# Attention masks per key block, two score rounds before two products with v, and an order of issue from a list scheduler

## The chip, the cores and the metric

The kernel runs on one core of a Trainium2 chip. The metric is device time in microseconds (us). A run of the kernel before takes 985 to 991 us, and the runs of one kernel mostly lie within 0.3% of their median (0.4% at most).

Engines in the profile: PE is TensorE's matrix products, PEld its weight loads, DVE is VectorE, ACT is ScalarE, POOL is GpSimd, SP is SyncE. A "q" after the name (SPq) is the engine's queue, which issues transfers.

## The reference, cut to what matters

```python
# attention: batch 4, 8 heads, 768 tokens, head size 64
q_bucket = sum over 6 bits of (q @ proj > 0) * 2**bit      # k_bucket likewise
scores = where(q_bucket == k_bucket, q @ k.T / 8, -1e9)
attn = exp(scores - max);  attn = attn / (sum(attn) + 1e-9)
x = attn @ v                                               # then (tokens, heads * 64)
# feed-forward: 3072 tokens, 512 -> 2048 -> 512
h = x @ w_in;  g = h * erf(softplus(h));  out = g @ w_out
```

The kernel does attention first (32 heads, two at a time: 16 pairs), then the feed-forward part. The mask is a matrix product too: bits of +1 and -1, with a large weight, are added into the scores before the exponential.

## The kernel before

A pair is four rounds `n`: two halves of the queries times two halves of the keys. A round has three key blocks `c` of 128 keys. All engines get their instructions in the order in which this program emits them, and each engine works its list off in that order; semaphores make an instruction wait for what it reads.

```python
def scores(n):                       # cut
    for part in range(2):            # part 0: masks, part 1: scores
        for c in range(GC):          # three key blocks
            for ab in range(2):      # the two heads of the pair
                rows = slice(ab * D, ab * D + D)
                ks, qs = d["k"][rows, :], d["q"][rows, :]
                if part == 0:
                    ks, qs = bit_rows(d, ab, c % 2)      # 32 rows of bits
                nc.tensor.matmul(out=d["st"][c][:, ab, 0:HS], lhsT=ks[:, keys], rhs=qs[:, cols],
                                 start=(part == 0), stop=(part == 1))
...
def invert(i):                       # after the divisor went through DRAM (zd, zc)
    nc.vector.reciprocal(out=zc, in_=zc)
    nc.sync.dma_start(out=rd..., in_=zc)
    for ab in range(2):              # spread over 64 rows each
        nc.sync.dma_start(out=d["r"][ab * D : ab * D + D, :], in_=rd[ab : ab + 1, :].broadcast_to([D, S]))

def normalise(i):                    # x = (x + ev) * r, on VectorE
    nc.vector.scalar_tensor_tensor(out=x, in0=x, scalar=d["ev"][:, 0:1], in1=d["r"], op0=ALU.add, op1=ALU.mult)
    nc.sync.dma_start(out=xs[b][j], in_=x)
...
for n in range(NS + 1):              # written out by hand, cut
    scores(n); exponentials(n)
    if ahead: hash_bits(pairs[i + 1], big)
    sum_keys(n - 1); weigh(n - 1)    # weigh: product with v of the round before
    if ahead: take_bits(pairs[i + 1], bitp)
    ...
    if r == 3 and i >= 1: invert(i - 1)
    if r == 1 and i >= 2: normalise(i - 2)
```

The divisor goes a long way: `z` leaves for DRAM as `zd`, comes back spread over 128 rows as `zc`, is inverted, leaves again as `rd`, and comes back as `r`, repeated for the 64 rows of each head. SyncE requests all four transfers.

Between these, ScalarE and VectorE convert the weights, one piece of 512 KB for every two rounds (`keep`, `top`, `unit`, `rest`), and VectorE adds up parts of them (presums).

Of the kernel before, what the change touches and what calls it, by code (L numbers as in the profile page):

```python
# [56 lines left out]
P = 128  # L58
# [88 lines left out]
def kernel(  # L147
# [36 lines left out]
    QR = 32  # L184
    proj_sb = const.tile([P, 2 * QR], F32, name="proj_sb")
    weight = const.tile([P, 1], F32, name="weight")
# [9 lines left out]
    most = const.tile([P, 2, B * H], F32, name="most")  # L196
    proj_in = const.tile([P, 2 * NBIT], F32, name="proj_in")
    nc.scalar.dma_start(out=proj_in, in_=proj2)
    nc.vector.memset(proj_sb, 0.0)
    for ab in range(2):  # L200
# [6 lines left out]
    nc.scalar.dma_start(out=row, in_=bucket)  # L207
    steps = const.tile([P, 3], F32, name="steps")
    nc.vector.tensor_scalar(
        out=steps[:, 0:1],  # L210
        in0=row,
        scalar1=float(QR),
        scalar2=-float(QR),
        op0=ALU.is_ge,
        op1=ALU.mult,
    )
    nc.vector.tensor_tensor(out=row, in0=row, in1=steps[:, 0:1], op=ALU.add)
    for c, (end, factor) in enumerate(((NBIT, NBIT + 1.0), (NBIT + 1, -float(NBIT)))):
        nc.vector.tensor_scalar(
            out=steps[:, c + 1 : c + 2],  # L220
            in0=row,
            scalar1=float(end),
            scalar2=factor * BIG,
            op0=ALU.is_lt,
            op1=ALU.mult,
        )
    nc.vector.tensor_tensor(out=weight, in0=steps[:, 1:2], in1=steps[:, 2:3], op=ALU.add)
    nc.vector.memset(ones, 1.0)
# [55 lines left out]
    def fetch(i, load):  # L284
        d = dict(
            q=load.tile([P, S], F32, name="q", tag="q"),
            k=load.tile([P, S], F32, name="k", tag="k"),
            v=load.tile([P, NC, P], F32, name="v", tag="v"),
        )
        b, j = divmod(i, JP)  # L290
        for n, what in enumerate("qk"):
            for ab in range(2):
                nc.sync.dma_start(
                    out=d[what][ab * D : ab * D + D, :],
                    in_=qkT[2 * i + ab, n * D : n * D + D, :],
                )
        for ab in range(2):
            nc.sync.dma_start(
                out=d["v"][:, :, ab * D : ab * D + D],
                in_=v[b, 2 * j + ab].rearrange("(c p) d -> p c d", p=P),  # L300
            )
        return d
# [14 lines left out]
    def take_bits(d, bitp, halves=(0, 1)):  # L317


        if halves[0] == 0:  # L320
            for what in ("qb", "kb"):
                d[what] = bitp.tile([P, S], BF16, name=what, tag=what)
        h0, h1 = halves[0], halves[-1] + 1
        cols = slice(h0 * HS, h1 * HS)
        nc.scalar.activation(
            out=d["qb"][:, cols].rearrange("p (h s) -> p h s", s=HS),
            in_=d["bits"][:, h0:h1, 0:HS],
# [4 lines left out]
        for half in (1, 0):  # L332
            nc.vector.tensor_scalar(
                out=d["kb"][half * D : half * D + D, cols],
                in0=d["qb"][D:P, cols],
                scalar1=weight[D:P, 0:1],
                scalar2=None,
                op0=ALU.mult,
            )
        nc.vector.tensor_copy(out=d["qb"][D:P, cols], in_=d["qb"][0:D, cols])  # L340

    def bit_rows(d, ab, copy):

        rows = slice(copy * D + ab * QR, copy * D + ab * QR + QR)
        return d["kb"][rows, :], d["qb"][rows, :]

    def attention():
        NS = NPAIR * 4
        with (
# [19 lines left out]
            def fetch_weights(n):  # L369
                if n >= len(pieces):  # L370
                    return
                queue = nc.sync if n < 2 else nc.gpsimd
# [8 lines left out]
            def round_weights(n, part):  # L381
# [5 lines left out]
                raw = raws[n]  # L387
                low, high = raw[:, :, 0], raw[:, :, 1]
                if part == 0:
                    keep = cvt.tile([P, WP], I32, name="keep", tag="keep")  # L390
                    top = cvt.tile([P, WP], I32, name="top", tag="top")
                    raws[n, 1] = keep, top
                    sq = keep[:, :].bitcast(F32)
                    nc.scalar.activation(out=sq, in_=high.bitcast(F32), func=AF.Square)  # L394
                    nc.scalar.activation(  # L395
                        out=keep, in_=sq, func=AF.Sign, scale=-1.0, bias=tiny2[:, 0:1]
                    )
                    nc.vector.tensor_scalar(
                        out=top,
                        in0=high,  # L400
                        scalar1=3,
                        scalar2=0x7FFFFFFF,
                        op0=ALU.logical_shift_left,
                        op1=ALU.bitwise_and,
                    )
                    nc.vector.scalar_tensor_tensor(
                        out=top,
                        in0=high,
                        scalar=SIGN,
                        in1=top,  # L410
                        op0=ALU.bitwise_and,
                        op1=ALU.bitwise_or,
                    )
                    return
                keep, top = raws.pop((n, 1))
                unit = cvt.tile([P, WP], I32, name="unit", tag="unit")
                rest = cvt.tile([P, WP], F32, name="rest", tag="rest")
# [4 lines left out]
                    in1=keep,  # L422
# [5 lines left out]
                )  # L428
                nc.vector.scalar_tensor_tensor(
# [10 lines left out]
                raws.pop(n)  # L440

            def scores(n):
# [3 lines left out]
                d["st"] = [big("st") for _ in range(GC)]  # L446
                for part in range(2):
                    for c in range(GC):
                        keys = slice((g * GC + c) * P, (g * GC + c + 1) * P)
                        for ab in range(2):  # L450
                            rows = slice(ab * D, ab * D + D)
                            ks, qs = d["k"][rows, :], d["q"][rows, :]
                            if part == 0:
                                ks, qs = bit_rows(d, ab, c % 2)
                            nc.tensor.matmul(  # L455
                                out=d["st"][c][:, ab, 0:HS],
                                lhsT=ks[:, keys],
                                rhs=qs[:, cols],
                                start=(part == 0),
                                stop=(part == 1),  # L460
                            )

            def exponentials(n):
                d = pairs[n // 4]
                for c, st in enumerate(d.pop("st")):
                    e = etiles[(n * GC + c) % len(etiles)]
                    nc.scalar.activation(  # L467
                        out=e[:, :, 0:HS], in_=st[:, :, 0:HS], func=AF.Exp, scale=scale
                    )

            def sum_keys(n):
                d = pairs[n // 4]
                key = "sum", n // 2 % 2
                es = [etiles[(n * GC + c) % len(etiles)][:, :, 0:HS] for c in range(GC)]
                if n % 2 == 0:
                    d[key] = sums.tile([P, 2, HS], F32, name="sum", tag="sum")
                    nc.vector.tensor_tensor(out=d[key], in0=es[0], in1=es[1], op=ALU.add)
                    es = es[2:]
                for e in es:
                    nc.vector.tensor_tensor(out=d[key], in0=d[key], in1=e, op=ALU.add)  # L480

            def weigh(n):
# [5 lines left out]
                for c in range(GC):  # L488
                    e = etiles[(n * GC + c) % len(etiles)]
# [13 lines left out]
            def divisor(n):  # L503
                half = n // 2 % 2
                d = pairs[n // 4]
                z = bank("z_ps")[:, 0:HS]
                for ab in range(2):
# [6 lines left out]
                    )  # L514
                if half == 0:
                    d["z"] = home(n // 4).tile([P, S], F32, name="z", tag="z")
                nc.scalar.copy(out=d["z"][:, half * HS : (half + 1) * HS], in_=z)

            def leave(n):

                half = n // 2 % 2
                d = pairs[n // 4]
                cols = slice(half * HS, (half + 1) * HS)
                if half == 0:
                    d["x"] = home(n // 4).tile([P, S], F32, name="x", tag="x", bufs=3 if n < NS - 4 else 1)
                nc.scalar.copy(out=d["x"][:, cols], in_=d["av"][:, 0:HS])
                if half == 0:
                    d["ev"] = small.tile([P, 1], F32, name="ev", tag="ev")
                    nc.vector.tensor_scalar(
                        out=d["ev"],  # L530
                        in0=d["av"][:, HS : HS + 1],
                        scalar1=EPS,
                        scalar2=None,
                        op0=ALU.mult,
                    )

            def spread(i):

                d = pairs[i]
                zd = dram.tile([2, S], F32, name="zd", tag="zd")  # L540
                d["zc"] = small.tile([P, 2 * S // P], F32, name="zc", tag="zc")
                for ab in range(2):
                    nc.sync.dma_start(out=zd[ab : ab + 1, :], in_=d["z"][ab * D : ab * D + 1, :])
                nc.sync.dma_start(
                    out=d["zc"],
                    in_=zd[:, :].rearrange("a (p c) -> (a p) c", c=2 * S // P),
                )

            def invert(i):
# [6 lines left out]
                rd = dram.tile([2, S], F32, name="rd", tag="rd")  # L556
# [685 lines left out]
```

## Time and profile before

| | before |
|---|---|
| median, us | 987 |
| attention: first mask to last product with v, us | 10.6 to 354.0 |
| one pair in the steady part, us | 21.38 |
| VectorE's busy time in a pair, us | 18.8 to 19.6 |
| ScalarE's, us | 14.1 |

The prediction below shows the busy shares, the stretches of two pairs and the order of time. A line of an order of time has the start in us, the length, the engine, the line of the program, the operation, out<-in, and in brackets how long the engine had been idle and what ended that.

The list of waits of the kernel before (engine, what it did, what it waited for: total us, times, longest) has it once in the whole run:

```profile
DVE x L571 <- DMA r<-rd: 1.5, 1, 1.5
```

### The profile page before, as it was taken

Reading aid. Unit: us, or ns where it says so; the run is one execution under the profiler, and the core shown is the slowest. Engines: PE = TensorE matmul, PEld = TensorE weight load, DVE = VectorE, ACT = ScalarE, POOL = GpSimd, SP = SyncE. Lnnn points to the kernel's source line nnn. Section 1 sums busy time; section 2 is a strip of 40 time slices with the busy share of each in tenths; the row PEclk is TensorE's granted clock in tenths of the full one; section 3 lists DMA queues with packets and bytes.
Section 4 is the critical chain, followed back from the end, with each engine's and each line's share of the span. In section 5 each row is a group of like instructions: output and inputs, shape, how many; then the busy total and the mean of one; then the engine's idle time right before and its main releaser. Section 6 shows DMA issues by size and latency. Waiting matters only on the chain.

```text
span 986.7 us, 11526 instructions
## 1 busy us (share of the span) xinstructions
PE 968.8 (98%) x4290; PEld 557.3 (56%) x4290; DVE 837.5 (85%) x1071; ACT 734.0 (74%) x866; POOL 16.2 (2%) x34
## 2 busy tenths in 40 slices
PE   7999999999999999999999999999999999999997
PEld 2444444444444467765666666666666666666543
DVE  3888898989998967989999999988998899888861
ACT  3676676666666637789889988988788889987960
POOL 0000000000000000000000000000000000000000
PEclk9999999999999999999999999999999999999999
DMA  8454556654555322211112102210221000000001
GB/s 187 111 126 124 145 140 154 144 160 125 126 144 139 120 92 80 76 33 32 49 46 88 33 28 85 70 33 16 75 74 33 1 22 22 1 1 21 22 1 45
DMA packets 61680, 74.54 MB, mean 76 GB/s; under 512 B 33936, under 2 KB 44176, under 8 KB 61616
## 3 DMA queue, kind: packets, MB, share of 16 engines
q1 hardware_dynamic: 57008, 57.99, 21.6%
q0 software_dynamic: 4320, 15.73, 5.3%
q8 instruction: 35, 0.57, 0.2%
q14 instruction: 29, 0.24, 0.1%
q10 hardware_dynamic: 288, 0.01, 0.0%
HBM read 60.92 MB, written 12.78 MB: 75 GB/s over the span
## 4 chain that ended last, share of the span: by engine, by line
PE 92%; ACT 4%; DVE 2%; issue 1%; DMA 1%; SPq 0%; DVEq 0%
PE o_ps L902 32%; PE X L791 16%; PE st L455 14%; PE av L492 13%; PE Z L791 8%; PE Y L791 4%; PE bits L309 3%; PE z_ps L508 2%; ACT e L467 1%; ACT keep L395 1%; ACT keep L394 1%; DVE s L876 1%; DMA k<-in_qkT_dram 0%; DVE s L852 0%; DVE s L846 0%
## 5 line engine op out<-in xcount | busy, mean ns | idle before, releaser
L902 PE MATMUL o_ps<-w_out_sb,h 128*128 128x512 f32 x768 | 341.5, 593 | 0.0
L902 PEld LDWEIGHTS o_ps<-w_out_sb,h 128*128 128x128 f32 x768 | 146.1, 190 | 152.7 <-issue 147.6
L467 ACT ACTIVATE e<-st 128x768 f32<-128x768 f32 x192 | 141.3, 808 | 29.6 <-PE st L455 28.7
L455 PE MATMUL st<-q,k 64*128 64x384 f32 x768 | 143.2, 506 | 0.0
L492 PE MATMUL av<-e,v 128*64 128x385 f32 (+1 forms) x768 | 138.3, 493 | 0.0
L480 DVE TENSOR_TENSOR sum<-sum,e 128x768 f32<-128x768 f32 x128 | 121.6, 950 | 7.4 <-DVE sum L480 0.5
L876 DVE SCALAR_TENSOR_TENSOR s<-q,s 128x1024 f32<-128x1024 f32 x96 | 116.4, 1221 | 8.9 <-ACT q L872 5.3
L872 ACT ACTIVATE q<-z,cq 128x1024 f32<-128x1024 f32 x96 | 105.8, 1143 | 1.4
L455 PEld LDWEIGHTS st<-q,k 64*128 64x128 f32 x768 | 69.7, 189 | 53.9 <-issue 21.5
L492 PEld LDWEIGHTS av<-e,v 128*64 128x64 f32 x768 | 56.7, 136 | 71.9 <-issue 62.1
L791 PE MATMUL X<-x,w_in_sb 128*128 128x256 f32 x384 | 90.6, 380 | 2.1 <-ACT h L805 1.6
L805 ACT COPY h<-X 128x512 f32<-128x512 f32 x96 | 55.2, 575 | 44.3 <-PE X L791 35.6
L791 PEld LDWEIGHTS X<-x,w_in_sb 128*128 128x128 f32 x384 | 72.9, 190 | 25.3 <-issue 12.1
L836 DVE SCALAR_TENSOR_TENSOR w<-w,e 128x1024 f32<-128x1024 f32 x48 | 58.4, 1223 | 17.6 <-ACT w L831 17.4
L846 DVE SCALAR_TENSOR_TENSOR s<-h,s 128x1024 f32<-128x1024 f32 x48 | 58.6, 1221 | 17.1 <-ACT s L842 17.1
L863 ACT ACTIVATE z<-s 128x1024 f32<-128x1024 f32 x48 | 50.5, 1052 | 29.0 <-DVE s L852 28.8
L891 DVE TENSOR_TENSOR h<-h,s 128x1024 f32<-128x1024 f32 x48 | 57.2, 1219 | 3.2 <-ACT s L887 3.2
L852 DVE SCALAR_TENSOR_TENSOR s<-s,w 128x1024 f32<-128x1024 f32 x48 | 58.7, 1222 | 1.2
L827 ACT ACTIVATE e<-e 128x1024 f32<-128x1024 f32 x48 | 50.4, 1049 | 10.6 <-DVE e L817 10.5
L876 DVE SCALAR_TENSOR_TENSOR s<-z,s 128x1024 f32<-128x1024 f32 x48 | 57.1, 1219 | 0.0
L872 ACT ACTIVATE z<-z,cq 128x1024 f32<-128x1024 f32 x48 | 53.4, 1141 | 0.1
L887 ACT ACTIVATE s<-s 128x1024 f32<-128x1024 f32 x48 | 49.2, 1052 | 4.7 <-DVE s L876 4.3
(79 smaller groups left out, 1173.6 us busy)
## 6 DMA issues: line engine op xcount, KB each, us to landing
t<-in_qkT_dram SPq DMA_DIRECT2D x64, 192.0 KB
raw<-in_w_out_dram POOLq DMA_DIRECT2D x16, 512.0 KB, 3.7
raw<-in_w_in_dram POOLq DMA_DIRECT2D x14, 512.0 KB, 3.9
q<-in_qkT_dram SPq DMA_DIRECT2D x32, 192.0 KB
k<-in_qkT_dram SPq DMA_DIRECT2D x32, 192.0 KB
v<-in_v_dram SPq DMA_DIRECT2D x32, 192.0 KB
r<-rd SPq DMA_DIRECT2D x32, 192.0 KB
xs<-x SPq DMA_DIRECT2D x16, 384.0 KB
```

Source lines behind the costliest of these rows:

```text
L455: nc.tensor.matmul(out=d["st"][c][:, ab, 0:HS], lhsT=ks[:, keys], rhs=qs[:, cols], start=(part == 0), stop=(part == 1),)
L467: nc.scalar.activation(out=e[:, :, 0:HS], in_=st[:, :, 0:HS], func=AF.Exp, scale=scale)
L480: nc.vector.tensor_tensor(out=d[key], in0=d[key], in1=e, op=ALU.add)
L492: nc.tensor.matmul(out=d["av"][rows, 0:w], lhsT=d["v"][:, g * GC + c, rows], rhs=e[:, ab, 0:w], start=(g == 0 and c == 0), stop=(g == 1 an ...
L791: nc.tensor.matmul(out=d[into][:, u, :], lhsT=a[:, kc, f : f + P], rhs=b[:, kc, :], start=(first and u == 0 and kc == 0), stop=(last and u ...
L836: nc.vector.scalar_tensor_tensor(out=w, in0=w, scalar=-1.0, in1=st[p]["e", u], op0=ALU.add, op1=ALU.subtract)
L846: nc.vector.scalar_tensor_tensor(out=s, in0=unit(p, u), scalar=0.0, in1=s, op0=ALU.max, op1=ALU.add)
L852: nc.vector.scalar_tensor_tensor(out=s, in0=s, scalar=S_MAX, in1=st[p].pop(("w", u)), op0=ALU.min, op1=ALU.subtract,)
L872: nc.scalar.activation(out=q, in_=z, func=AF.Square, bias=cq[:, j : j + 1])
L876: nc.vector.scalar_tensor_tensor(out=s, in0=st[p].pop(("q", u, j)), scalar=ERF_Q[j][1], in1=s, op0=ALU.add, op1=ALU.mult,)
L891: nc.vector.tensor_tensor(out=h, in0=h, in1=st[p].pop(("s", u)), op=ALU.mult)
L902: nc.tensor.matmul(out=o_live[tt], lhsT=st[p]["h"][:, u, 2 * fh + half, sub * P : (sub + 1) * P], rhs=w_out_sb[:, fh * NF // 2 + 2 * c + u ...
```

## The change

The intent: TensorE changes the shape of its array less often, starts sooner, and the order of issue on all engines comes from a list scheduler with a table of durations.

```diff
-        nc.vector ... scalar1=weight[D:P, 0:1]            # one weight, 32-row bits, two copies
+        nc.vector ... scalar1=weight[D:P, ab : ab + 1]    # a weight per head, 64 rows, zeros for the other head
-            def scores(n):         # three masks, then three scores
+            def score(n, c):       # mask and score of one key block
+                for part, src in enumerate(("b", "")):
+                    for ab in range(2):
+                        rows = slice(ab * D, ab * D + D)
+                        nc.tensor.matmul(out=st[:, ab, 0:HS], lhsT=d["k" + src][rows, keys],
+                                         rhs=d["q" + src][rows, cols], start=(part == 0), stop=(part == 1))
...
-            for n in range(NS + 1):    # the order by hand
+            for h in range(NH):
+                order += [("score", n) for n in (2 * h + 1, 2 * h + 2) if n < NS]
+                if h % 2 == 0 and h // 2 + 1 < NPAIR:
+                    order.append(("bits", h // 2 + 1))
+                if h >= 1:
+                    order.append(("divisor", h - 1))
+                order += [("weigh", 2 * h), ("weigh", 2 * h + 1)]
...
+                op(spread, (i,), "SP", 0.8, (0, n, 0), (("keep_divisor", 2 * i + 1),), late=2.0)
+                op(gather, (i,), "SP", 0.35, (0, n, 1), (("spread", i),), late=2.0)
+                op(invert, (i,), "DVE", 0.4, (0, n + 8, 3), (("gather", i),))
+                op(ungather, (i,), "SP", 0.35, (0, n, 2), (("invert", i),), late=2.0)
+                op(widen, (i,), "SP", 1.1, (0, n, 3), (("ungather", i), ("send", i - 1)), late=2.2)
+                op(normalise, (i,), "DVE", 0.95, (0, n + 8, 4), (("widen", i), ("leave", 2 * i + 1)))
+                op(send, (i,), "SP", 0.35, (0, n, 4), (("normalise", i),), late=2.2)
...
+            for each in arrange(ops, {}):
+                each.emit()
...
-                queue = nc.sync if n < 2 else nc.gpsimd    # weight pieces
+                queue = nc.gpsimd
+    WARM = 7                                               # products of ones, to open the clock
```

In an `op` line the numbers are the assumed duration, the rank, and `late`, the assumed time until another engine sees the result. They only decide the order in which instructions are emitted. Also in the diff: the first pair's q and k come in halves, part of them from ScalarE's queue; x has two buffers in place of three.

## The prediction

> **What bounds the kernel now.** I read the page first (busy shares, chain, costliest groups), then stretches, then the order of time in one steady pair of heads and in the start. Page, busy shares and chain:
>
> ```profile
> PE 968.8 (98%) x4290; PEld 557.3 (56%) x4290; DVE 837.5 (85%) x1071; ACT 734.0 (74%) x866; POOL 16.2 (2%) x34
> PE 92%; ACT 4%; DVE 2%; issue 1%; DMA 1%; SPq 0%; DVEq 0%
> ```
>
> TensorE sets the end. So an instruction saved elsewhere is worth nothing; a gap or boundary inside TensorE's stream is worth its full length. Attention runs from 10.61 us (first mask product) to about 354.0 us (the first feed-forward product follows at 354.55 us); the rest, 632 us, is the same code after the change. Two consecutive pair periods (columns: stretch; busy us of PE, PEld, DVE, ACT, POOL; clock; DMA):
>
> ```profile
> 191.33:212.71 21.38, 21.33 (x138) 9.76 (x136) 18.80 (x30) 14.06 (x21) 1.06 (x2) 1.00 0.54 138
> 212.71:234.09 21.38, 21.33 (x138) 9.76 (x136) 19.62 (x30) 14.04 (x21) 1.05 (x2) 1.00 0.56 143
> ```
>
> A pair takes 21.38 us, TensorE never waits, VectorE is at 88 to 92%, ScalarE at 66%. Order of time on TensorE in the first of them:
>
> ```profile
> 193.03 0.89 PE L508 MATMUL z_ps<-sum,ones 128*64 128x384 f32 x4
> 193.84 0.50 PE L455 MATMUL st<-qb,kb 32*128 32x384 bf16 x6
> 194.27 2.21 PE L455 MATMUL st<-q,k 64*128 64x384 f32 x12
> 196.41 2.16 PE L492 MATMUL av<-e,v 128*64 128x385 f32 x12
> 198.50 0.50 PE L455 MATMUL st<-qb,kb 32*128 32x384 bf16 x6
> ```
>
> Three shapes of the array take turns: 32 rows by 128 columns (masks), 64 by 128 (scores), 128 by 64 (products with v, bits, divisor). Starts give the costs: masks 0.43 (194.27-193.84), scores 2.14, products 2.09 us. Instructions run two at a time, and inside a run a pair starts every 0.323 us (weight loads of one run start at 25.71, 26.03, 26.36, 26.68 us). Six pairs are then 1.94 us: 0.20 of 2.14 and 0.15 of 2.09 are boundary. In raw starts, the last pair before a change of shape lasts 0.418 instead of 0.323 (+0.095), and the first pair after it runs 0.105 longer for 128-column f32 weights (587 ns recorded, 482 otherwise) and 0.052 for 64-column ones.
>
> The start (order of time):
>
> ```profile
> 2.00 1.23 SPq L293 DMA_DIRECT2D k<-in_qkT_dram  x2
> 5.10 1.51 PE L309 MATMUL bits<-q,proj_sb 128*64 128x384 f32 x2 [5.10 <-DVE weight L227]
> 6.95 1.51 PE L309 MATMUL bits<-k,proj_sb 128*64 128x384 f32 x2 [0.33 <-DMA k<-in_qkT_dram]
> 11.79 4.21 PE L455 MATMUL st<-q,k 64*128 64x384 f32 x12
> ```
>
> The first bits wait for whole q and k; twelve score products take 4.21 us here against 2.21 later. That is a half-rate clock; the trace's first full-clock record is at 17.1 us (the page's clock row doesn't show it).
>
> **What the Trainium skill says.** "TensorEngine Tiling (Array Packing)", Key Properties: changing tiling mode drains TensorE, changing tile doesn't. Agrees: 0.095 us at each change of shape. "TensorE: Matmul & The Clock Gate", LDWEIGHTS: time goes with columns, P/1.2 ns, so 107 ns for 128 and 53 for 64. Agrees with 105 and 52 exposed above. Same page, Part 1: the clock is at half until about 3.4 us of sustained activity, in a free-running window. Agrees with the slow start. "Trainium Kernel Development and Optimization", Key Constraints: more issuing queues only save issue time; here SyncE issues one transfer per 0.6 us, so that saving is real at the start.
>
> **The change, part by part.**
>
> 1. Order and mask shape. Before, a pair has 4 rounds of masks, scores, products: 12 changes of shape. After, masks use 64 rows like the scores, and each half does two score blocks (six key blocks), bits if due, divisor, two products: 2 changes per half, 4 per pair. New key block: one mask pair, 384 columns at the rate of the f32 pair (which streams twice) 0.161 us, plus two score pairs 0.645 = 0.81 (the scheduler's own table says 0.82). The next f32 weights need 0.107 us and fit under the mask pair, if that load isn't held back by the change of type; no run shows such a pair yet. Per pair: 12 x 0.81 = 9.72; products 24 x 0.323 = 7.75; bits four pairs 1.29; divisor 2 x 0.645 = 1.29; per half one change into the products (0.095 + 0.052) and one out (0.095, and some 0.03 that I guess for the first mask load), 0.27, twice 0.54. Sum 20.59; with the table's 0.82 for a key block, 20.71. I take 20.67. Against 21.38 that is 0.71 per pair, 16 pairs: **11.4 us**, all on the path.
>
> 2. Start. Halves of q and k come first, two of them from ScalarE's queue. Before, a 196 KB transfer landed 3.3 us after issue; the k second half is issued last, at about 3.75 us (six SyncE issues of 0.6 us), and lands at about 7.1. TensorE is in order and does these bits before the first score: first mask about 7.8 instead of 10.61, **2.8 us**. The seven warm products (512 columns at half clock, 0.43 us each, 3.0 us in all, from about 1.25) end just before first data. If they open the clock (I give 60%), about 3 us of half-rate work in the old start also go; if not, some 0.3 us. The mean is 1.9.
>
> 3. VectorE and ScalarE do the same operations. Weight conversion, presums and first-block presums move by rank. VectorE's 18.8 to 19.6 us in 20.67 is 91 to 95%. The schedule assumes DMA delays shorter than the trace: small transfers zc and rd take 3.3 and 3.4 us from issue (medians) against 2.35. VectorE, in order, may block about 1 us at the reciprocal and again at the normalise, nearly all its slack of 1.1 to 1.9. But sums are used about 7 us after their exponentials, so I allow TensorE only 1 us in all.
>
> 4. Feed-forward: unchanged, 0 +- 1.
>
> End of attention: 7.8 + 16 x 20.67 - 1.29 (no bits in the last pair) - 0.65 (last divisor comes later) = 336.6, + 1.1 remaining cold clock + 1 stalls = 338.7 against 354.0: 15.3 us. 987.6 - 15.3 = **972.3**.
>
> **Rivals.** (a) *VectorE becomes the bound.* At 95% plus blocked waits it would set a pair at about 21.0 to 21.4 us: total 978 to 984. For it: the utilisations and short assumed delays. Against it: the group list shows sums waiting only 0.5 us on anything in the old order. (b) *Type changes cost what shape changes did.* Each half now has six mask-to-score turns; at 0.1 us each that is 1.2 per pair, and the gain of part 1 vanishes: about 984 to 990. For it: the old mask-to-score turn did cost 0.2. Against it: the drain goes with shape by the skill, and 0.105 is the load after a drain. (c) *Everything works*: clock opens early, no stalls, and the 2.8 us of TensorE waits between 354 and 392 us (0.58, 1.56 and 0.67 in the order of time) shrink since VectorE comes in with less work: 966 to 968. (d) *The start is hidden anyway*: k's second half lands late and scores start at 9.5: 974.
>
> **Range and chances.** Part 1 is nearly exact unless (b); the start has +-2, stalls +3, the feed-forward's start +-1. Range 967 to 979. Faster by over 2% needs below 967.8: only (c), 0.13. Slower by over 2% would need a blocked queue: 0.02. Within 2%: 0.85.
>
> **What will show it.** Step 1: the six-block score run lasts 4.9 us (5.5 under (b)), pair period 20.6 to 20.8 with TensorE busy throughout. Step 2: first mask near 7.8 us, its scores spaced 0.32 (warm) or 0.64 (cold). Step 3: VectorE shows waits on zc and r, TensorE none on sums or exponentials. Step 4: feed-forward span again 632. The prediction is wrong if the period stays at 21 or more, if gaps appear ahead of scores, or if the feed-forward start moves by more than 2 us.

## More of the kernel before

```profile
209.23 1.10 SPq L562 DMA_DIRECT2D r<-rd  x2
...
217.46 1.01 DVE L571 SCALAR_TENSOR_TENSOR x<-x,ev,r 128x768 f32<-128x768 f32 x1
```

The normalise comes 8.2 us after the request, without a bracket: `r` was there.

## The result, and the profile after

The changed kernel takes 1009.45 us (median of 4 runs, 1007.85 to 1010.55), the kernel before 986.98 us in the same rounds. The ratio is 1.0227, interval 1.0205 to 1.0249: slower by 2.3%. (A ratio here is the mean time of one kernel's fast runs over that of the other's in the same rounds, so it isn't quite the ratio of the medians.) Executions over 1.5% slower than the fastest of the same kernel are left out of the means. Attention ends 21.7 us later than before; the feed-forward part, 632 us before, takes 631 us.

The page of the changed kernel, busy shares and the chain that ended last:

```profile
PE 970.6 (96%) x4297; PEld 562.1 (56%) x4297; DVE 836.7 (83%) x1074; ACT 735.0 (73%) x866; POOL 18.0 (2%) x37
...
PE 76%; DVE 13%; DMA 6%; ACT 2%; issue 2%; SPq 1%; DVEq 0%
```

The chain was 92% TensorE and 1% DMA; now VectorE and transfers hold 19% of it. VectorE does no more work than before (837 us), so the question is when it stands still. Two stretches of one pair each (columns: stretch; busy us of PE, PEld, DVE, ACT, POOL; clock; DMA share; GB/s), one before the trouble, one in it:

```profile
41.00:61.50 20.50, 20.50 (x138) 9.72 (x136) 16.30 (x27) 13.86 (x22) 1.06 (x2) 1.00 0.33 98
...
125.00:154.80 29.80, 22.85 (x140) 10.60 (x138) 26.01 (x39) 15.09 (x23) 1.58 (x3) 0.94 0.49 137
```

The first is what the change was for: 20.5 us per pair and TensorE full. From start of bits to start of bits, undisturbed pairs take 20.53 us, against 21.38. The second takes 29.8 us; TensorE stands still for 7 us of it, and the clock column says 0.94. Of the last 13 intervals between pairs four kept 20.53 us; the 13 together are 33 us too long, and a gap of 2.5 us follows in the last pair. (A gap in this text runs from the start of one product to the start of the next; the idle times in brackets begin at the product's end and are some 0.5 us shorter.) The list of waits:

```profile
DVE x L614 <- DMA r<-rd: 42.8, 15, 3.9
ACT keep L403 <- DVE top L439: 25.3, 13, 3.8
PE st L479 <- ACT e L493: 15.3, 7, 3.7
PE st L479 <- DVE kb L340: 6.3, 2, 3.4
```

VectorE now waits for `r` once per pair, 2.85 us on the mean. The order of time shows how this reaches TensorE:

```profile
116.43 0.35 SPq L597 DMA_DIRECT2D rd<-zc  x1
...
119.77 1.61 SPq L606 DMA_DIRECT2D r<-rd  x2
...
124.16 1.02 DVE L614 SCALAR_TENSOR_TENSOR x<-x,ev,r 128x768 f32<-128x768 f32 x1 [3.75 <-DMA r<-rd]
...
127.03 0.69 DVE L439 SCALAR_TENSOR_TENSOR top<-top,keep 128x512 int32<-128x512 int32 x1
127.75 0.71 ACT L403 ACTIVATE keep<-raw 128x512 f32<-128x512 f32 x1 [3.47 <-DVE top L439]
128.37 1.48 ACT L493 ACTIVATE e<-st 128x768 f32<-128x768 f32 x2
...
131.15 0.46 ACT L548 COPY z<-z_ps 128x384 f32<-128x384 f32 x1
...
133.61 1.22 DVE L635 TENSOR_TENSOR w_in_sb<-w_in_sb 128x1024 f32<-128x1024 f32 x1
134.75 1.22 DVE L635 TENSOR_TENSOR w_sum<-w_in_sb,w_sum 128x1024 f32<-128x1024 f32 x1
135.98 0.85 DVE L340 TENSOR_SCALAR kb<-qb,weight 64x768 bf16<-64x768 bf16 x2
136.87 0.35 DVE L350 COPY qb<-qb 64x768 bf16<-64x768 bf16 x1
136.89 0.70 PE L479 MATMUL st<-qb,kb 64*128 64x384 bf16 x2 [3.36 <-DVE kb L340]
```

Read it from the top. `rd` is sent at 116.43 us, `r` is requested once that has landed, at 119.77 us, and VectorE reaches the normalise at 120.4 us and stands there 3.75 us. ScalarE's next square needs the one `keep` buffer, which VectorE hasn't freed, so ScalarE stands too, with two exponentials behind the square. The divisor's copy, behind these on ScalarE, comes at 131.15 us, 4.5 us after its last product began (0.7 us in an undisturbed pair), which delays the next `r`. VectorE meanwhile works off its list in the fixed order, two presums included, before it reaches the bits `kb` of the next pair. TensorE has stood for 3.36 us by then. The Trainium skill ("TensorE: Matmul & The Clock Gate", Part 1) calls ACT and DVE strict FIFO, and the trace agrees: nothing behind the normalise starts on VectorE in these 3.75 us.

A second loss follows. The trace's clock records show half rate for five stretches between 138 and 302 us, 20.5 us in all. Each begins in a gap of 3.4 us or more in TensorE, or within 1.4 us after it. In them the bits' products start 0.64 us apart, against 0.32 us otherwise, so these stretches cost up to 10 us (an estimate: half of 20.5).

The start of the changed kernel:

```profile
1.40 4.45 PE L642 MATMUL warm<-w_sum 128*128 128x512 bf16 x7 [1.40 <-DVE w_sum L200]
...
1.91 1.05 POOL L389 DMA_DIRECT2D raw<-in_w_in_dram  x2
...
5.78 0.90 PE L316 MATMUL bits<-q,proj_sb 128*64 128x384 f32 x1
...
9.69 0.87 PE L316 MATMUL bits<-q,proj_sb 128*64 128x384 f32 x1 [1.95 <-DMA q<-in_qkT_dram]
...
11.53 0.50 PE L479 MATMUL st<-qb,kb 64*128 64x384 bf16 x2
```

The first mask comes at 11.53 us, 0.9 us later than before, not 2.8 us earlier. The seven warm products took 4.45 us and the clock opened only at 15.3 us. GpSimd asks for 1 MB of weights at 1.91 us, in the middle of the loads of q and k.

### The profile page after: what moved, and what is told of

Same layout as the page of the kernel before. It is cut to its first block, busy times and chain, and to the rows that moved or that the text cites. A ratio compares the mean times of both kernels' runs of the same rounds, so it can differ in the third digit from the quotient of the medians.

```text
span 1007.4 us, 11511 instructions
## 1 busy us (share of the span) xinstructions
PE 970.6 (96%) x4297; PEld 562.1 (56%) x4297; DVE 836.7 (83%) x1074; ACT 735.0 (73%) x866; POOL 18.0 (2%) x37
## 4 chain that ended last, share of the span: by engine, by line
PE 76%; DVE 13%; DMA 6%; ACT 2%; issue 2%; SPq 1%; DVEq 0%
PE o_ps L1081 31%; PE X L970 16%; PE st L479 8%; PE Z L970 8%; PE av L519 7%; DVE sum L505 4%; PE Y L970 4%; DMA r<-rd 3%; DMA rd<-zc 2%; PE bits L316 2%; PE z_ps L536 1%; DVE top L439 1%; DVE rest L457 1%; ACT e L493 1%; DVE s L1055 1%
## 5 line engine op out<-in xcount | busy, mean ns | idle before, releaser
L493 ACT ACTIVATE e<-st 128x768 f32<-128x768 f32 x192 | 149.6, 812 | 25.0 <-PE st L479 25.0
L479 PE MATMUL st<-q,k 64*128 64x384 f32 x768 | 161.1, 497 | 0.0
L519 PE MATMUL av<-e,v 128*64 128x385 f32 (+1 forms) x768 | 129.8, 487 | 2.0 <-DVE ev L563 2.0
L984 ACT COPY h<-X 128x512 f32<-128x512 f32 x96 | 55.2, 575 | 42.8 <-PE X L970 35.6
L479 PE MATMUL st<-qb,kb 64*128 64x384 bf16 x384 | 65.5, 332 | 21.6 <-ACT e L493 15.3
L557 ACT COPY x<-av 128x384 f32<-128x384 f32 x32 | 15.3, 478 | 85.0 <-PE av L519 85.0
L1025 DVE SCALAR_TENSOR_TENSOR s<-h,s 128x1024 f32<-128x1024 f32 x48 | 58.6, 1221 | 17.1 <-ACT s L1021 17.1
L479 PEld LDWEIGHTS <-kb 64*128 64x128 bf16 x384 | 20.3, 95 | 67.3 <-issue 39.5
```

The lines of the kernel that those rows point to most:

```text
L479: nc.tensor.matmul(out=st[:, ab, 0:HS], lhsT=d["k" + src][rows, keys], rhs=d["q" + src][rows, cols], start=(part == 0), stop=(part == 1),)
L493: nc.scalar.activation(out=e[:, :, 0:HS], in_=st[:, :, 0:HS], func=AF.Exp, scale=scale)
L519: nc.tensor.matmul(out=d["av"][rows, 0:w], lhsT=d["v"][:, g * GC + c, rows], rhs=e[:, ab, 0:w], start=(g == 0 and c == 0), stop=(g == 1 an ...
L1025: nc.vector.scalar_tensor_tensor(out=s, in0=unit(p, u), scalar=0.0, in1=s, op0=ALU.max, op1=ALU.add)
```

## The experiments

Theory A: VectorE, in order, stands at the normalise until `r` lands, and this alone costs what the new order gained and more. Rivals: B, VectorE has too much work for a 20.5 us pair; C, ScalarE's wait for `keep` is the link that matters; and an order that is bad apart from this wait. Each kernel ran with a profile and 3 or 5 rounds against the kernel before on the same chip. Unless said otherwise the edit is to the changed kernel, and the outputs were correct.

**No wait for r (wrong result).**

```diff
-  out=x, in0=x, scalar=d["ev"][:, 0:1], in1=d["r"], op0=ALU.add, op1=ALU.mult
+  out=x, in0=x, scalar=d["ev"][:, 0:1], in1=x, op0=ALU.add, op1=ALU.mult
```

> Wrong result on purpose: the normalise multiplies by x in place of r, so every engine has the order of the changed kernel unaltered and only the wait for r at this place is gone. Theory A: like e1, 972 to 977. If it is the new order on the queues that is bad (for instance kb behind presums), and not the wait: waits of TensorE on kb and e stay, over 995.

Measured: 973.74 us, ratio to before 0.9856 (0.9837 to 0.9876). Every engine has the same list in the same order, every transfer is still made, only the normalise no longer reads `r`. Two stretches of about a pair, columns as above:

```profile
122.10:142.60 20.50, 20.50 (x138) 9.61 (x136) 19.63 (x30) 14.20 (x22) 1.06 (x2) 1.00 0.47 133
142.60:163.20 20.60, 20.60 (x140) 9.75 (x138) 19.68 (x31) 14.01 (x22) 1.06 (x2) 1.00 0.55 143
```

TensorE is full while VectorE works 96% of the time, so rival B falls. Between 13.7 and 969 us no clock record shows half rate. The wait at `r` costs 1009.5 - 973.7 = 35.7 us (36.7 by the two ratios). This run shows theory A as far as one run can.

**Late normalise.**

```diff
-  op(normalise, (i,), ..., (("widen", i), ("leave", 2 * i + 1)))
+  op(normalise, (i,), ..., (("widen", i), ("leave", 2 * i + 1), ("score", 4 * i + 9, 2)))
```

> Only the normalise of a pair is moved later in VectorE's order (it may follow the score block of three rounds on). Theory A (VectorE, which is in order, stands at the normalise until r lands, 2.3 to 3.9 us per pair in the trace of the changed kernel, and everything behind it is late): the waits on r go, a pair takes 20.5 us throughout as it did between 25 and 75 us, the clock isn't lowered any more, total 972 to 977. Rival B (VectorE has simply too much work for a 20.5 us pair): the idle time on r goes but pairs stay at 21.2 us or more, total over 985. Rival C (ScalarE's square waiting for the one keep buffer holds back the exponentials): little change, over 1000.

Measured: 979.2 us, ratio 0.9918 (0.9894 to 0.9942): a right result, faster than before, but 2 us outside what A expected. The 42.8 us of waits at `r` shrank to one of 1.5 us, and ten of the last 13 intervals between pairs were 20.53 us. Two gaps of about 2 us were left, at 224 and 309 us; at the first, ScalarE's square had waited 1.8 us for VectorE. The list of waits also has VectorE at `zc`, five times, 6.2 us in all.

**Two buffers for keep.**

```diff
-  keep = cvt.tile([P, WP], I32, name="keep", tag="keep")
+  keep = cvt.tile([P, WP], I32, name="keep", tag="keep", bufs=2)
```

> Two buffers for keep, so that ScalarE's square need not wait for VectorE's mask of the piece before (25 us in 13 waits in the changed kernel). Theory A: VectorE still stands 2.8 us per pair at r, so TensorE's gaps stay for the most part: 998 to 1008. Rival C: the gaps go with ScalarE's waits, 972 to 985.

Measured: 1011.34 us, ratio 1.0224 (1.0199 to 1.025), the same as without, and 3 us above what A expected. Its list of waits:

```profile
DVE x L614 <- DMA r<-rd: 46.4, 15, 4.5
...
PE st L479 <- DVE kb L340: 19.8, 11, 4.6
```

ScalarE's wait for `keep` is no longer among those listed, and TensorE now waits for `kb` directly, which VectorE makes. Rival C falls: ScalarE passed the delay on but wasn't its source.

**First two weight pieces on SyncE.**

```diff
-  queue = nc.gpsimd
+  queue = nc.sync if n < 2 else nc.gpsimd
```

> The first two weight pieces (1 MB) go back to SyncE's queue, behind the loads of the first pairs; in the changed kernel GpSimd starts them at 1.9 us, among the loads of q and k. If they are what made q and k late (bits at 5.8 and 9.7 us where I had 4.5 and 7.1), the first mask comes at 8 to 9.5 us in place of 11.5 and the total falls by 2 to 4 us, to about 1006. Rival: the halved loads or ScalarE's queue are slow by themselves: first mask stays after 11 us, total unchanged.

Measured: 1007.21 us, ratio 1.0195 (1.0169 to 1.0221). In the trace the first mask came at 9.58 us in place of 11.53 (8 to 9.5 had been expected). The total fell by the expected 2 us, which is little more than the scatter of the runs; the trace is the better witness.

**Late normalise, two keep buffers, weight pieces on SyncE.** (The three edits above together.)

> The late normalise of the first experiment, with two buffers for keep and the first two weight pieces on SyncE's queue. With the late normalise alone two gaps of 2 us were left in TensorE, at 224 and 309 us, behind ScalarE's square that waited 1.8 us for VectorE's mask of the piece before. If that is their cause, two buffers, which did nothing while VectorE stood at r, take them away now, and the start gains its 2 us: 979 less 3.5 less 2, so 972 to 975, all pairs at 20.5 us. If the gaps have another cause (VectorE's load): pairs over 20.5 remain and the total is 976 or more.

Measured: 978.17 us, ratio 0.9904 (0.9882 to 0.9926): a miss, 3 us over. The two gaps of 2 us were gone, but one of 4.9 us had come at 190 us, with half clock from 192 to 199 us. SyncE's waits in this kernel, and the order of time around the gap:

```profile
SPq L620 <- DVE x L614: 99.0, 16, 8.1
```

```profile
167.89 0.64 SPq L577 DMA_DIRECT2D zd<-z  x2
...
177.33 0.17 DVE L589 TENSOR_SCALAR zc<-zc 128x12 f32<-128x12 f32 x1 [4.01 <-DMA zc<-zd]
...
179.36 1.10 SPq L606 DMA_DIRECT2D r<-rd  x2
...
188.62 0.33 SPq L620 DMA_DIRECT2D xs<-x  x1
189.04 1.12 SPq L300 DMA_DIRECT2D q<-in_qkT_dram  x2
...
192.75 0.64 SPq L577 DMA_DIRECT2D zd<-z  x2
```

SyncE is in order as well. It stands at the store of x (`send`) until the late normalise is done at 188.6 us, and the divisor's way out (`zd`), ready at 184.3 us, leaves at 192.75 us. That is after the gap; the same delay one pair earlier came before it. There `zd` left at 167.89 us, 4.6 us after its copy, and VectorE stood at `zc` for 4.01 us, until 177.33 us. The wait had moved from VectorE's list to SyncE's.

**Send later.** The late normalise and the weight pieces on SyncE stay, and:

```diff
-  op(send, (i,), ..., (("normalise", i),), late=2.2)
+  op(send, (i,), ..., (("normalise", i), ("spread", i + 1)), late=2.2)
-  d["x"] = home(i).tile([P, S], F32, name="x", tag="x")
+  d["x"] = home(i).tile([P, S], F32, name="x", tag="x", bufs=3 if i < NPAIR - 1 else 1)
```

> In the three-mends kernel the one gap of 4.9 us at 190 us came from SyncE's order: the store of x waits there for the late normalise (up to 8.1 us) and holds back the loads of a later pair and the divisor's zd behind it (zd 0.5 us after its copy at first, 8.9 us by the eighth pair), so that VectorE stands at zc. Here the normalise stays late, the first two weight pieces stay on SyncE, the store of x comes behind the next pair's zd, with three buffers for x (one for keep again, for want of room). If that explanation holds: zd follows its copy by about 0.5 us in all pairs, no wait on zc, all pairs 20.5 us, total 970 to 973. If not: gaps of 2 to 5 us stay, 976 or more.

Measured: 971.35 us, ratio 0.9825 (0.9811 to 0.9839), as expected. `zd` follows its copy by 0.5 us in every pair, and every pair of the steady part takes 20.53 us, with one `keep` buffer.

**Dense warm products.** The kernel above, with:

```diff
-    WARM = 7
+    WARM = 9
+  warm_ps = bank("warm")          # taken once
-      out=bank("warm"),           # in the loop
+      out=warm_ps,
```

> The send-later kernel with nine warm products into one buffer taken once, in place of seven that each take the buffer anew and so wait for the one before (0.64 us apart where 0.43 would be the rate). If the gaps between them are what keeps the clock low, it opens at or before the first bits (5.3 to 6.8 us) and the first scores run 0.32 us apart: 1 to 2 us less than the send-later kernel, 969 to 971. If all-ones operands or something else keep it low, no difference beyond 0.5 us.

Measured: 968.52 us, ratio 0.9799 (0.9786 to 0.9813), the fastest of all. Its start:

```profile
1.40 3.88 PE L645 MATMUL warm<-w_sum 128*128 128x512 bf16 x9 [1.40 <-DVE w_sum L200]
...
6.79 0.54 PE L316 MATMUL bits<-q,proj_sb 128*64 128x384 f32 x1 [0.71 <-ACT qb L329]
7.66 0.43 PE L479 MATMUL st<-qb,kb 64*128 64x384 bf16 x2
```

Nine products take less time than seven that wait for one another, the clock opens at 5.0 us (at 7.3 us in the send-later trace), and the first mask comes at 7.66 us (8.90). The edit changes the number of products and their spacing together, and no run separates the two.

**No warm products.** The send-later kernel with `WARM = 0`.

> The send-later kernel without warm products. The seventh of them started at 5.26 us, just when q was there, and held the bits back 0.5 us; the clock rose only at 11 to 15 us with them. If they are useless: same or up to 1 us less. If they help in part of the runs: 0 to 2 us more.

Measured: 970.94 us, ratio 0.9824 (0.981 to 0.9838): no difference from seven spaced ones. The clock opened at 11.3 us in its trace. As the change has them, the warm products are worth nothing that can be measured; dense ones are worth 2.4 to 2.8 us.

**Delays as traced.**

```diff
-  spread ... late=2.0 | gather ... late=2.0 | ungather ... late=2.0 | widen ... late=2.2
+  spread ... late=2.6 | gather ... late=3.0 | ungather ... late=3.1 | widen ... late=3.0
```

> The changed kernel, with only the scheduler's assumed delays of the chain from divisor to r set near those of the trace of the kernel before (zd 2.6, zc 3.0, rd 3.1, r 3.0 us in place of 2.0, 2.0, 2.0, 2.2); 3.5 us in all, where VectorE stood 2.8 us per pair. Theory A with the cause in the table's numbers: VectorE's waits at r fall below 1 us per pair, most of TensorE's gaps go, 974 to 984, and no lowered clock. If the cause is not these numbers but that VectorE runs behind the table for other reasons: waits of 2 us and more stay, over 995.

Measured: 988.16 us, ratio 0.9999 (0.9968 to 1.003): a miss, between the two expectations.

```profile
DVE x L614 <- DMA r<-rd: 20.9, 15, 3.4
```

Half of the waiting is left, and so is about 40% of the loss. Waits at `r` of 42.8, 20.9 and 0 us went with 1009.5, 988.2 and 973.7 us. Why only half, the scheduler's own code tells:

```python
away = 0.0 if names[a].engine == engine else names[a].late    # in arrange
```

`late` isn't added where the next step is on the same engine. `spread` and `gather` are both SyncE's, and so are `ungather` and `widen`. So the table lets SyncE ask for `r` 0.35 us after it has sent `rd`, as if `rd` had landed by then. `arrange`, run by itself on the table of kernel.py, gives the same order even with 9.0 us as `late` of `spread` and `ungather`: two of the four new numbers did nothing, and only those of `zc` and `r` worked.

This accounts for the wait in the changed kernel. Its table puts the normalise 3.75 us after the sending of `rd` (12 of 15 pairs), and in the trace VectorE gets there 3.8 us after (median): it isn't late. The transfers are. On the mean, `r` is requested 2.70 us after `rd` is sent, and VectorE starts the normalise 4.08 us after that request (0.35 and 3.50 in the table). That is 2.9 us more than the table has, and VectorE stands 2.85 us. No run mends that line of the scheduler, so this last step rests on table and trace.

**One by one.** The late-normalise kernel with score rounds and products taking turns singly, as the kernel before does:

```diff
-  order: score, score, (bits), divisor, weigh, weigh
+  order: score, (bits), weigh, score, divisor, weigh
```

> The late normalise of the first experiment, but score rounds and products with v take turns one by one as in the kernel before, in place of two and two. Eight changes of shape per pair in place of four. By the prediction's figures (0.095 + 0.052 into the products, 0.095 + some 0.03 out) a pair takes 0.54 us more, 21.05 us, and the total is 979 + 8.6 = 986 to 990, less up to 3.5 if the two leftover gaps vanish with the longer pair. If the order were worth nothing by itself: 979.

Measured: 986.75 us, ratio 0.9994 (0.9967 to 1.0022). A stretch of one pair:

```profile
100.60:121.70 21.10, 21.10 (x140) 9.34 (x138) 20.17 (x29) 15.04 (x22) 0.53 (x1) 1.00 0.59 152
```

From bits to bits an undisturbed pair takes 21.05 us, which is 0.52 us more than 20.53, for four changes of shape more. So the order of two and two is worth 0.52 us per pair. (One gap of 4.2 us came at 217 us, after VectorE had stood at a late `zc` for 4.57 us until 201.9 us, so the total doesn't isolate it; the pair does.)

**Masks only.** The kernel before, with 64-row masks per key block and nothing else of the change:

```diff
-  for part in range(2):
-      for c in range(GC):
+  for c in range(GC):
+      for part in range(2):
-  rows = slice(copy * D + ab * QR, copy * D + ab * QR + QR)
+  rows = slice(ab * D, ab * D + D)      # and a weight per head, as in the change
```

> The kernel before with the mask part alone: 64-row masks per key block, its own order and start. By the prediction's sum a round's masks and scores become 3 x 0.81 + 0.095 = 2.52 instead of 2.56 us: one change of shape of three is gone, but masks lose their four at a time. So a pair goes from 21.38 to about 21.2 us and the total to 984 to 987. If type changes cost what shape changes do (rival b of the prediction), it is slower than before, over 989.

Measured: 984.92 us, ratio 0.9977 (0.9957 to 0.9997). A pair takes 21.27 us. This part is worth 0.11 us per pair by itself.

**The old order, normalise one round earlier.** The kernel before, with:

```diff
-  if r == 1 and i >= 2:
+  if r == 0 and i >= 2 and n < NS:
       normalise(i - 2)
```

> The kernel before, with the normalise of a pair one round earlier in VectorE's order, right behind the round in which r is asked for; nothing else. r then lands some 2 to 3 us after VectorE gets there. Theory A: VectorE (19.2 us of work per 21.38 us pair) can't make up 2.5 us of standing still, pairs grow to 21.7 or more, total 992 to 1010, perhaps with a lowered clock. If standing at r is harmless as long as TensorE's stream is the old one: 986 to 990.

Measured: 1024.14 us, ratio 1.0384 (1.0354 to 1.0415).

```profile
DVE x L571 <- DMA r<-rd: 53.1, 15, 5.1
```

One moved instruction per pair makes the old kernel slower than the changed one, with the same sign in the list of waits and half-rate stretches in the clock records. It cost more than A had put down (992 to 1010). The mistake needs neither the scheduler nor the new shape.

## Why the prediction was wrong

The loss comes from one step, the third: "VectorE, in order, may block about 1 us at the reciprocal and again at the normalise, nearly all its slack of 1.1 to 1.9. But sums are used about 7 us after their exponentials, so I allow TensorE only 1 us in all." The wait was seen, but its cost was mis-sized: 35.7 us in place of 1.

- **Size of the wait.** There was none to speak of at the reciprocal, and 2.85 us per pair at the normalise. The prediction held the delays of `zc` and `rd` in the old order (3.3 and 3.4 us) against 2.35 us in the table for each. For `zc` that is what the table has, but in the new order `zc` landed after 1.6 us (median), before VectorE came. For `rd` the table has 0.35 us, because both requests are SyncE's, where the trace has 2.70; `r` itself added another 0.6. This rule of the scheduler was overlooked.
- **What a wait costs an engine that is 96% busy.** 19.6 us of work and 2.85 of standing still don't go into 20.53 us. I compared the wait with VectorE's slack, found them about equal, and still booked it as hidden. A deficit adds up from pair to pair: the last sum of a half started 0.6 to 2.1 us after its exponential in the first two pairs, and up to 9.7 us after it in the sixth.
- **The wrong consumer.** I checked the sums, and these were in fact ready 7 us or more before TensorE used them, up to 361 us. TensorE was stopped through `kb` and through ScalarE's square, both behind the normalise in a fixed order, and then slowed by the lowered clock, which the prediction considered at the start only.
- **Rival (a)** was the right mechanism ("VectorE becomes the bound", with blocked waits), mis-sized at 978 to 984 us; slower by over 2% through "a blocked queue" had been given a chance of 0.02. Its reason against, that the old order's sums hardly waited, was no evidence: a list of waits of one order says nothing of another.
- **Part 1 held.** Predicted 20.67 us per pair, measured 20.53. The entry and exit costs came out as put: 0.54 us per pair for four changes of shape predicted, 0.52 measured. Rival (b), that type changes cost as much, fell: in the raw starts the score pair follows its mask pair after 0.16 us.
- **Part 2 failed on its own.** First mask predicted at 7.8 us, measured 11.53. I had overlooked that all weight pieces now go to GpSimd's queue; the scheduler's "after the sums" only orders the emission, and GpSimd started at 1.9 us. I had taken 3.3 us from request to landing from the first of four loads before; the fourth took 4.2 us there, and the last half of k 6.1 us in the changed kernel. I also took the warm products to be 0.43 us apart; they wait for each other and were 0.64 apart. With both mended the first mask came at 7.66 us.
- **Part 4 held.** The feed-forward part took 631 us.

With the wait taken away the changed kernel ran in 973.7 us where the prediction had 972.3; this is close partly because the better pairs made up for the start.

What stays open: how the 35.7 us divide between waiting and half clock, and what the changed kernel would take if the scheduler counted the landing of `zd` and `rd`.

## What to carry to other kernels

Before you shorten the stream of the engine that bounds, add up busy time plus waits of the next one in the new period: at 96% busy a wait of 3 us per period isn't hidden, it accumulates. On engines that work in order, put an instruction that needs a transfer well behind the time at which the data lands, and then look at what stands behind it in the queue of the engine that stores its result. A scheduler's "after" is no wait at run time, and its assumed delays deserve the same check against a trace as its durations; check too that they are counted between two transfers that the same engine requests.

## What the Trainium skill lacked or had wrong

- "TensorEngine Tiling (Array Packing)", Key Properties, says that a change of shape drains TensorE but gives no size. Here it is 0.095 us of lengthened spacing at full clock, plus exposed weight loads of 0.05 to 0.10 us; four changes fewer per pair gave 21.05 to 20.53 us.
- No page that I found says what a change from bf16 masks to f32 scores in the same shape costs. Here nothing shows: the f32 pair starts 0.16 us after the bf16 pair of 384 columns.
- "TensorE: Matmul & The Clock Gate", Part 1, asks for sustained activity to open the clock but doesn't say how dense. Seven warm products 0.64 us apart left it closed until 6.8 to 15.6 us in nine traces (without any it opened at 8.3 to 17.1 us in four); with nine without waits between them it opened at 5.0 us in the one trace of them. It gives about 3.4 us of idleness before the clock falls. In the changed kernel only gaps of 3.4 us or more brought half rate, which agrees; in the keep experiment one gap of 2.6 us was followed by it, and in the early-normalise experiment one of 4.3 us wasn't, so it isn't a sharp limit.
